# Exchanging two ScalarE instructions in the first chunk: square root of tile 2 ahead of tile 1's second-half evacuation

## The chip, the cores and the metric

The kernel runs on one core of one Trainium2 chip. The metric is the device time of one execution in microseconds (us). The six executions of the kernel before that the result is measured against lie between 180.17 and 180.61 us, within 0.24% of one another. The effect studied here is about that size (0.34%), so the experiments were timed in five rounds against the kernel before on the same chip, and the trace was read as well as the clock. The granted clock is the share of full speed that the profile records for TensorE; its mean is listed with every execution.

Engines: TensorE (PE in the profile; PEld is its weight load), VectorE (DVE), ScalarE (ACT), GpSimd (POOL), SyncE (SP).

## The reference

```
xn  = layernorm(x)                                    # x: 1 x 2048 x 512, bf16
A   = S5 state-space layer on xn (complex scan over 2048 steps)
B   = (silu(xn @ w_gate) * (xn @ w_up)) @ w_down      # hidden width 1376
out = x + A(xn) + B(xn)
```

The kernel takes the 2048 rows in four chunks of 512. Only the start of the first chunk matters here. Its four tiles of 128 rows (tile 0 to tile 3) are normalised and transposed, and TensorE multiplies each with the gate weights as soon as it is ready.

## The kernel before

The program records tasks in a graph, and a static list scheduler orders the tasks of ScalarE, VectorE and GpSimd from estimates of their durations. TensorE and SyncE keep the order in which they were recorded. Each engine is then given its list in that order. An `order` (`od`) entry constrains the scheduler only. It adds no semaphore, since it joins tasks of one engine.

For each tile, VectorE computes the statistics, ScalarE takes the square root of the variance, and VectorE takes the reciprocal and normalises in two halves of 256 columns:

```python
def ln_stat0(a, order):
    t = g.add("dve", lambda e: e.bn_aggr(out=mv[:, a, :], ...))
    hold["sd%d" % a] = g.add("act", lambda e: e.activation(out=sd0[:, a:a + 1], in_=mv[:, a, 1:2], func=AF.Sqrt, bias=epst[:, 0:1]), ...)
...
# VectorE's order in chunk 0: r reciprocal, n normalise half h, b statistics of half h, s aggregate (and ScalarE's square root)
for op, a, h in (("r", 0, 0), ("n", 0, 0), ("b", 1, 0), ("b", 1, 1), ("s", 1, 0), ("n", 0, 1), ("b", 2, 0),
                 ("r", 1, 0), ("n", 1, 0), ("n", 1, 1), ("b", 2, 1), ("s", 2, 0), ("b", 3, 0),
                 ("r", 2, 0), ("n", 2, 0), ("n", 2, 1), ("b", 3, 1), ("s", 3, 0), ...
```

Each half tile is transposed by TensorE into PSUM (line 569 of the program) and brought back to SBUF by ScalarE (line 581), or by VectorE for tile 3. The gate matmuls (line 785) read it there. The transposes are interleaved with the matmuls of the previous half:

```python
for q in range(4):                                   # q: tile
    for k0, k1 in ...((0, 2), (2, 4)):               # half of the contraction
        for n, (i, bk) in enumerate(tiles):          # seven gate tiles
            if k0 == 0 and n == (2 if q == 0 else 1):
                xt_tile_fine(q, 1)                   # two transposes, then evacuation ev<q>1
            if k0 == 2 and n == 1 and q < 3:
                xt_tile_fine(q + 1, 0)               # two transposes, then evacuation ev<q+1>0
            ...                                      # two matmuls of 128 columns
```

ScalarE's own order in this stretch is written out. `sd` is a square root and `ev` an evacuation, with tile and half:

```python
seq = ["sd0", "ev00", "sd1", "ev01", "ev10", "ev11", "sd2", "ev20", "sd3", "ev21"]
for a_, b_ in zip(seq, seq[1:]):
    hold[b_].od.add(hold[a_])
```

## Time and profile before

| | before |
|---|---|
| median of 3 runs | 180.33 us (180.17 to 180.47) |
| span in the profile | 178.5 us |
| TensorE, VectorE, ScalarE busy | 98%, 91%, 49% |
| TensorE's share of the chain that ended last | 97% |

The first two lines are from the profile's page: busy time by engine, and the shares of the chain that ended last, by engine.

```profile
PE 174.5 (98%) x936; PEld 83.8 (47%) x936; DVE 163.1 (91%) x285; ACT 87.5 (49%) x110; POOL 11.3 (6%) x21
...
PE 97%; ACT 1%; DVE 0%; issue 0%
```

So in this kernel a microsecond saved on VectorE or ScalarE should be worth nothing unless TensorE waits for it. TensorE's waits fit in three lines. One of them belongs here (engine, line, releaser: total us, times, longest):

```profile
PE pb L569 <- DVE xn_sb L514: 0.5, 1, 0.5
```

The chain of waits of the kernel before, around that place (start, duration, what):

```profile
8.10 0.13 PE pb L569 x2
...
8.24 0.38 ACT xnT L581
8.63 0.19 ACT sd L521
...
8.84 0.18 DVE rstd L529
...
9.04 0.36 DVE xn_sb L514
...
9.45 0.28 PE pb L569 x2
9.73 0.78 PE pb L785 x14
```

The chain leaves TensorE at 8.24, passes through ScalarE twice and VectorE twice, and comes back at 9.45. After that it stays on TensorE until the last output addition at 176.19. The same stretch in the timeline, and its last output addition (start, duration, engine, line, operation; in brackets the engine's idle time just before and its releaser):

```profile
7.50 0.21 DVE L519 BATCH_NORM_AGGREGATE mv<-st 128x2 f32<-128x12 f32 x1
...
7.93 0.28 PE L569 MATMUL pb<-ident,xn_sb 128*128 128x128 bf16 x2
...
8.24 0.38 ACT L581 ACTIVATE xnT<-pb 128x256 bf16<-128x256 bf16 x1 [0.57 <-PE pb L569]
8.52 0.29 ACT L521 ACTIVATE sd<-mv,epst 128x1 f32<-128x1 f32 x1
8.84 0.17 DVE L529 RECIPROCAL rstd<-sd 128x1 f32<-128x1 f32 x1 [0.84 <-ACT sd L521]
9.04 0.60 DVE L514 TENSOR_SCALAR xn_sb<-x_sb,mv,rstd 128x256 bf16<-128x256 bf16 x2
...
9.45 0.28 PE L569 MATMUL pb<-ident,xn_sb 128*128 128x128 bf16 x2 [0.46 <-DVE xn_sb L514]
...
10.35 0.28 PE L569 MATMUL pb<-ident,xn_sb 128*128 128x128 bf16 x2
...
176.19 0.29 DVE L958 TENSOR_TENSOR x_sb<-pb,x_sb 128x128 bf16<-128x128 f32 x1 [0.15 <-PE pb L953]
```

Tile 2's variance is complete at 7.50 + 0.21 = 7.71 us, but its square root (line 521) starts only at 8.52. Nothing in its own data holds it there. It stands in ScalarE's list behind the evacuation (the copy from PSUM to SBUF) at 8.24, which must wait for transposes that TensorE started at 7.93.

The cost is read from the starts of the transposes. From 9.45 to 10.35 TensorE needed 0.90 us for two transposes and 14 matmuls. From 7.93 to 9.45 it needed 1.52 us for the same work. The stall is therefore 0.62 us, although the list of waits counts 0.5: it counts from the modelled end of the matmul before, and in the records matmuls overlap (those of line 785 last 0.22 us each, but the 16 of a step start 0.90 / 16 = 0.056 us apart).

### The profile page before, as it was taken

To read this page: it belongs to the slowest core of one execution; us is meant where nothing else is said; L and a number is where in the kernel's file an instruction comes from. 1 tells how busy PE (TensorE), PEld (TensorE's weight loads), DVE (VectorE), ACT (ScalarE), POOL (GpSimd) and SP (SyncE) were. 2 spreads that over 40 slices of the span, in tenths; PEclk is the share of its full clock that TensorE was granted. 3 is DMA by queue.
4 is the path that set the end of the run, shared out by engine and by line. 5 is a ranking of instruction groups with operands and counts; after the bars stand their busy time and mean duration, and the time that the engine had idled before them with its cause. 6 is when DMAs were issued, how large, how long until landed. Compare 5 with 4: busy or idle time off the path is not lost.

```text
span 178.5 us, 2422 instructions
## 1 busy us (share of the span) xinstructions
PE 174.5 (98%) x936; PEld 83.8 (47%) x936; DVE 163.1 (91%) x285; ACT 87.5 (49%) x110; POOL 11.3 (6%) x21
## 2 busy tenths in 40 slices
PE   8989999999999999999999999999999999999994
PEld 2785444444444444444444444444444444444743
DVE  2768988997999999999999999999899999999933
ACT  4459999799999765024565651000965620000000
POOL 3014200130000000260000000000000000000000
PEclk9999999999999999999999999999999999999999
DMA  5995563569450000001510000001000000001022
GB/s 169 376 326 118 119 121 119 128 133 333 131 94 0 0 0 0 0 29 62 123 26 0 0 0 4 0 29 59 29 0 4 0 0 0 0 0 49 14 88 88
DMA packets 22978, 12.37 MB, mean 69 GB/s; under 512 B 15192, under 2 KB 22968, under 8 KB 22968
## 3 DMA queue, kind: packets, MB, share of 16 engines
q1 hardware_dynamic: 22472, 11.54, 23.6%
q10 hardware_dynamic: 496, 0.69, 1.1%
q8 instruction: 7, 0.11, 0.3%
q14 instruction: 3, 0.02, 0.0%
HBM read 6.46 MB, written 2.10 MB: 48 GB/s over the span
## 4 chain that ended last, share of the span: by engine, by line
PE 97%; ACT 1%; DVE 0%; issue 0%
PE pb L743 35%; PE pb L940 21%; PE pb L953 16%; PE pb L857 15%; PE pb L785 3%; PE pb L474 2%; PE pb L820 2%; PE pb L830 1%; PE pb L569 1%; ACT xnT L581 0%; DVE xn_sb L514 0%; DVE x_sb L958 0%; ACT sd L521 0%; DVE rstd L529 0%; PE pb L566 0%
## 5 line engine op out<-in xcount | busy, mean ns | idle before, releaser
L897 DVE TENSOR_TENSOR_SCAN rot<-sm,car,rot 128x512 bf16<-128x512 f32 x32 | 39.0, 1267 | 0.1
L940 PE MATMUL pb<-wd,hT 128*128 128x512 bf16 (+3 forms) x198 | 38.8, 356 | 0.0
L743 PE MATMUL pb<-xnT,wu 128*128 128x512 bf16 x160 | 37.3, 379 | 0.0
L743 PE MATMUL pb<-xnT,wg 128*128 128x512 bf16 x132 | 31.3, 380 | 0.0
L953 PE MATMUL pb<-W,hss 128*128 128x512 bf16 (+2 forms) x144 | 28.3, 356 | 0.0
L857 PE MATMUL pb<-xnT,BT 128*128 128x512 bf16 x128 | 28.1, 379 | 0.0
L940 PEld LDWEIGHTS pb<-wd,hT 128*128 128x128 bf16 (+1 forms) x198 | 18.5, 97 | 19.9
L755 ACT ACTIVATE sg<-pb 128x1024 bf16<-128x1024 f32 x20 | 20.1, 1024 | 9.2 <-PE pb L743 8.1
L743 PEld LDWEIGHTS pb<-xnT,wu 128*128 128x128 bf16 x160 | 15.6, 98 | 18.9 <-issue 0.2
L810 ACT ACTIVATE uf<-pb 128x1024 bf16<-128x1024 f32 x20 | 20.5, 1027 | 7.2 <-PE pb L743 6.1
L953 PEld LDWEIGHTS pb<-W,hss 128*128 128x128 bf16 x144 | 13.4, 98 | 14.3
L743 PEld LDWEIGHTS pb<-xnT,wg 128*128 128x128 bf16 x132 | 12.7, 98 | 15.7 <-issue 0.4
L857 PEld LDWEIGHTS pb<-xnT,BT 128*128 128x128 bf16 x128 | 12.5, 98 | 15.1
L864 ACT ACTIVATE u_sb<-pb 128x1024 bf16<-128x1024 f32 x16 | 16.2, 1021 | 5.9 <-PE pb L857 5.5
L958 DVE TENSOR_TENSOR x_sb<-pb,x_sb 128x512 bf16<-128x512 f32 (+2 forms) x18 | 11.1, 623 | 3.5 <-PE pb L953 3.5
L812 DVE TENSOR_TENSOR hT<-sg,uf 128x1024 bf16<-128x1024 bf16 x20 | 13.5, 684 | 0.6 <-ACT uf L810 0.5
L503 ACT ACTIVATE xn_sb<-x_sb,nmr,rstd 128x512 bf16<-128x512 bf16 x8 | 6.0, 803 | 9.7 <-DVE nmr L500 9.7
L839 ACT ACTIVATE sg<-pb 96x1024 bf16<-96x1024 f32 x2 | 2.0, 1020 | 17.1 <-PE pb L820 17.1
L888 DVE TENSOR_TENSOR rot<-u_sb,cosT 128x2048 bf16<-128x2048 bf16 x8 | 9.8, 1221 | 0.4 <-ACT u_sb L864 0.4
L888 DVE TENSOR_TENSOR rot<-rot,cosT 128x2048 bf16<-128x2048 bf16 x8 | 9.7, 1217 | 0.1
L888 DVE TENSOR_TENSOR rot<-u_sb,sin 128x2048 bf16<-128x2048 bf16 x8 | 9.8, 1220 | 0.0
L888 DVE TENSOR_TENSOR rot<-rot,sin 128x2048 bf16<-128x2048 bf16 x8 | 9.7, 1217 | 0.0
(78 smaller groups left out, 143.1 us busy)
## 6 DMA issues: line engine op xcount, KB each, us to landing
out_dram<-x_sb SPq DMA_DIRECT2D x15, 128.0 KB, 1.7
x_sb<-in_A_x_dram SPq DMA_DIRECT2D x3, 512.0 KB, 7.3
wd<-in_B_w_down_dram SPq DMA_DIRECT2D x1, 1280.0 KB, 6.8
wu<-in_B_w_up_dram SPq DMA_DIRECT2D x1, 768.0 KB, 5.0
wu<-in_B_w_up_dram SPq DMA_DIRECT2D x1, 608.0 KB, 7.2
x_sb<-in_A_x_dram SPq DMA_DIRECT2D x4, 128.0 KB, 3.4
wg<-in_B_w_gate_dram SPq DMA_DIRECT2D x1, 480.0 KB, 6.0
wg<-in_B_w_gate_dram ACTq DMA_DIRECT2D x1, 448.0 KB, 3.7
```

The source lines that it names most:

```text
L503: g.add("act", lambda e, a=a: e.activation(out=xn_sb[:, a % NXN, :], in_=x_sb[:, a, :], func=AF.Identity, scale=rstd[:, a:a + 1], bias=nmr ...
L743: inst = e.matmul(pbank[0:fs, bk, :].rearrange("p (j t) -> p j t", j=4), lhsT=w[:, kt, i * 128:i * 128 + fs], rhs=xnT[:, c % 2, :, kt, :], ...
L755: g.add("act", lambda e: e.activation(out=sg[rows, sl, 0:n, :].rearrange("p a t -> p (a t)"), in_=pair_f32(rows, bk, 512 * n), func=AF.Sil ...
L810: g.add("act", lambda e: e.activation(out=uf[rows, ul, 0:n, :].rearrange("p a t -> p (a t)"), in_=pair_f32(rows, bk, 512 * n), func=AF.Ide ...
L812: g.add("dve", lambda e: e.tensor_tensor(out=hT[rows, hb, i0:i0 + n, :], in0=sg[rows, sl, 0:n, :], in1=uf[rows, ul, 0:n, :], op=ALU.mult), ...
L857: inst = e.matmul(pbank[:, bk, :].rearrange("p (j t) -> p j t", j=4), lhsT=BT[:, ri, kt, pt * 128:(pt + 1) * 128], rhs=xnT[:, c % 2, :, kt ...
L864: g.add("act", lambda e: e.activation(out=u_sb[:, us].rearrange("p r t -> p (r t)"), in_=pair_f32(slice(0, 128), b0), func=AF.Identity), r ...
L888: tt = lambda out, a, b, op, r, w, nm: g.add("dve", lambda e: e.tensor_tensor(out=out, in0=a, in1=b, op=op), reads=r, writes=w, name="%s_% ...
L897: g.add("dve", lambda e, A0=A0, A1=A1, k=k, ri=ri, pt=pt: e.tensor_tensor_scan(out=A1[:, k, ri, :], data0=rr[:, pt:pt + 1].to_broadcast([1 ...
L940: inst = e.matmul(pbank[:, bk, 0:nc_], lhsT=hT[0:fs, hb, i, lt * 128:(lt + 1) * 128], rhs=wd[0:fs, i, c0:c0 + nc_], start=(i == 0), stop=F ...
L953: inst = e.matmul(pbank[:, bk, 0:nc_], lhsT=hss[:, hb, pt, ri, lt * 128:(lt + 1) * 128], rhs=W12[:, ri, pt, c0:c0 + nc_], start=False, sto ...
L958: g.add("dve", lambda e, bk=bk, a=a, c0=c0, nc_=nc_: e.tensor_tensor(out=x_sb[:, a, c0:c0 + nc_], in0=pbank[:, bk, 0:nc_], in1=x_sb[:, a, ...
```

## The change

The intent is to let ScalarE do first what can start first, namely the square root of tile 2 in the gap before the evacuation.

```diff
-            seq = ["sd0", "ev00", "sd1", "ev01", "ev10", "ev11", "sd2", "ev20", "sd3", "ev21"]
+            seq = ["sd0", "ev00", "sd1", "ev01", "ev10", "sd2", "ev11", "ev20", "sd3", "ev21"]
```

The scheduler sees other estimated times because of it and also moves some small work between 13 and 33 us. On VectorE three small operations and a piece of table arithmetic move; on ScalarE a sine table goes ahead of a Silu, and tiny sine evaluations change places. TensorE, GpSimd and SyncE keep their order. The diff of the source doesn't show these moves; they come from comparing the scheduled instruction lists.

## The prediction

> **What bounds the kernel now.** TensorE. The page gives it 174.5 of 178.5 us busy (98%), and the chain of waits that ended last is 97% TensorE, unbroken from 9.45 us to 176.17 us. VectorE is 91% busy, ScalarE 49%. The granted clock is 1.00 in every stretch. Its last detour is the one that the change touches: evacuation of tile 1's second half (ScalarE, 8.24), square root of tile 2 (8.52), reciprocal (VectorE, 8.84), normalisation of tile 2's first half (9.04), its transposes on TensorE (9.45).
>
> **The stall, from the timeline.** Transposes start at 6.98, 7.93, 9.45, 10.35, 11.24 us. A half-step without waiting (two transposes, 14 matmuls of 128 columns) therefore takes 0.89 to 0.90 us, 56 ns a matmul[...]. The step 7.93 to 9.45 took 1.52 us: 1.52 - 0.90 = 0.62 us of stall. (The list of waits counts 0.46 us, from the modelled end of the last matmul.)
>
> **What the change does.** No work is removed or added; two ScalarE instructions swap. Tile 2's variance is ready at 7.71, ScalarE is idle from 7.67 to 8.24, and the square root stands behind an evacuation that needs transposes begun at 7.93. Steps measured for the other tiles: aggregate start to square root start 0.24, to reciprocal 0.32, to normalisation 0.20, to transposes 0.40. From the aggregate at 7.50:
> - square root 7.74 (before 8.52), done by about 8.03 and so before the evacuation's 8.24, which is not delayed (0.29 us long in the trace);
> - reciprocal 8.06, normalisation 8.26, transposes possible from 8.66. TensorE reaches them at 7.93 + 0.90 = 8.83, so the stall vanishes entirely.
>
> Next link, tile 3: statistics 8.78, aggregate 9.24, square root 9.48 (behind an evacuation at 9.14), normalisation 10.00, transposes possible 10.40; TensorE arrives at 10.62. No new stall.
>
> **Does it survive?** From 9.45 on TensorE waits for nothing, so the 0.62 us should carry to the end unless something with less slack is fixed in time. Chunk 1's input landing (13.77) is fixed, and VectorE's statistics and the DMA transposes queue behind it. But TensorE needs the second weight transpose (landed about 22.1) only at 25.14; the last scaled weights (70.7) at 75.5; the last chunk's states (166.3) at 169.0. All slacks exceed 0.62 us. The static scheduler also reorders small work between 13 and 33 us (a few small VectorE products earlier, one table step ahead of chunk 1's normalisation, one sine table ahead of a Silu); I expect no effect on time, since chunk 1's DMA transpose stays bound by its queue at 22.2 us.
>
> **Prediction.** 180.33 - 0.62 = 179.7 us; 8 in 10: 179.45 to 180.05. Faster by over 2%: 0.01; within 2%: 0.985; slower: 0.005.
>
> **What would show it.** Square root of tile 2 near 7.74; transposes near 8.83 with no TensorE wait for the normalised tile; the later transposes spaced 0.90; feed-forward matmuls starting near 13.3 instead of 13.92; first Silu near 12.9; chunk 1's statistics still near 13.77; span near 177.9.
>
> **What would make it wrong.** Tile 3's chain arriving after 10.62, giving part back (its estimated margin is 0.22 us); the evacuation delayed by the square root; the reordered sine or table step delaying a Silu or a PSUM release and stalling TensorE between 14 and 30 us; DMA arrivals that TensorE now meets 0.62 us too early.

The 0.89 to 0.90 us of a half-step are read from the trace. The queue that holds chunk 1's DMA transpose to 22.2 us is in the trace: SyncE issued DMA transposes at 13.98, 18.11 and 22.23 us, and before the second and the third it waited 2.1 and 2.0 us for the landing of the one before.

## The result

| | before | after |
|---|---|---|
| median of 6 runs | 180.30 us (180.17 to 180.61) | 179.64 us (179.53 to 180.06) |
| ratio | | 0.9966 (95%: 0.9952 to 0.9981) |
| span in the profile | 178.5 us | 177.8 us |
| tile 2's first transposes after tile 1's last | 1.52 us | 0.89 us |
| first 512-column matmul starts | 13.92 us | 13.20 us |

A ratio is the mean time of one kernel's runs over that of the other's of the same rounds, so it is not quite the ratio of the medians quoted. The difference is clear of noise, and inside the 2%.

The page of the kernel after, the same two lines:

```profile
PE 173.5 (98%) x928; PEld 83.8 (47%) x936; DVE 163.1 (92%) x285; ACT 87.5 (49%) x110; POOL 9.2 (5%) x21
...
PE 95%; DMA 1%; DVE 1%; issue 0%; ACT 0%
```

The smaller TensorE share of the chain is no new wait. In this execution the eleven matmuls of a constant that TensorE runs first (line 474) ran shorter (3.78 instead of 4.21 us), so the chain begins at the first input's DMA and not with them. TensorE also shows 928 matmul records instead of 936, with 936 weight loads in both; eight are missing from the trace.

The timeline of the kernel after, for the lines shown of before:

```profile
7.42 0.21 DVE L519 BATCH_NORM_AGGREGATE mv<-st 128x2 f32<-128x12 f32 x1
...
7.67 0.29 ACT L521 ACTIVATE sd<-mv,epst 128x1 f32<-128x1 f32 x1
...
7.85 0.28 PE L569 MATMUL pb<-ident,xn_sb 128*128 128x128 bf16 x2
...
7.99 0.16 DVE L529 RECIPROCAL rstd<-sd 128x1 f32<-128x1 f32 x1
8.16 0.38 ACT L581 ACTIVATE xnT<-pb 128x256 bf16<-128x256 bf16 x1 [0.20 <-PE pb L569]
8.19 0.60 DVE L514 TENSOR_SCALAR xn_sb<-x_sb,mv,rstd 128x256 bf16<-128x256 bf16 x2
...
8.74 0.28 PE L569 MATMUL pb<-ident,xn_sb 128*128 128x128 bf16 x2
...
9.63 0.28 PE L569 MATMUL pb<-ident,xn_sb 128*128 128x128 bf16 x2
...
175.48 0.29 DVE L958 TENSOR_TENSOR x_sb<-pb,x_sb 128x128 bf16<-128x128 f32 x1 [0.15 <-PE pb L953]
```

The whole execution starts 0.08 us earlier (7.85 for 7.93), because the first input landed earlier (the first statistics start at 3.08 and not at 3.17). With that taken off, the square root moved from 8.52 to 7.75. The evacuation that it overtook runs from 8.16, which is 8.24 on the old scale: not delayed at all. The transposes of tile 2 follow those of tile 1 by 8.74 - 7.85 = 0.89 us, and the next two by 0.89 again. The chain of waits no longer leaves TensorE here:

```profile
8.01 0.11 PE pb L569 x2
8.12 0.78 PE pb L785 x14
8.90 0.11 PE pb L569 x2
9.02 0.78 PE pb L785 x14
```

The list of TensorE's waits still has a line of the same name:

```profile
PE pb L569 <- DVE xn_sb L514: 0.3, 1, 0.3
```

It is another instance. The timeline shows that this is tile 0's, at the start, where the shorter run of those first matmuls exposed a wait that was there before:

```profile
4.96 0.28 PE L569 MATMUL pb<-ident,xn_sb 128*128 128x128 bf16 x2 [0.35 <-DVE xn_sb L514]
```

A group in a list of waits is a line of the program, not one place in time.

### The profile page after: what moved, and what is told of

It reads as the page before. It is cut to its first block, busy times and chain, and to the rows that moved or that the text cites. A ratio compares the mean times of both kernels' runs of the same rounds, so it can differ in the third digit from the quotient of the medians.

```text
span 177.8 us, 2415 instructions
## 1 busy us (share of the span) xinstructions
PE 173.5 (98%) x928; PEld 83.8 (47%) x936; DVE 163.1 (92%) x285; ACT 87.5 (49%) x110; POOL 9.2 (5%) x21
## 4 chain that ended last, share of the span: by engine, by line
PE 95%; DMA 1%; DVE 1%; issue 0%; ACT 0%
PE pb L743 36%; PE pb L940 21%; PE pb L857 16%; PE pb L953 15%; PE pb L785 4%; PE pb L820 2%; DMA x_sb<-in_A_x_dram 1%; PE pb L830 1%; PE pb L569 1%; DVE st L527 0%; ACT xnT L581 0%; DVE xn_sb L514 0%; ACT sd L521 0%; DVE x_sb L958 0%; DVE mv L519 0%
## 5 line engine op out<-in xcount | busy, mean ns | idle before, releaser
L940 PE MATMUL pb<-wd,hT 128*128 128x512 bf16 (+3 forms) x194 | 38.1, 355 | 0.2
L743 PEld LDWEIGHTS pb<-xnT,wg 128*128 128x128 bf16 x132 | 12.7, 98 | 15.7 <-issue 0.8
```

The source lines that it names most:

```text
L743: inst = e.matmul(pbank[0:fs, bk, :].rearrange("p (j t) -> p j t", j=4), lhsT=w[:, kt, i * 128:i * 128 + fs], rhs=xnT[:, c % 2, :, kt, :], ...
L940: inst = e.matmul(pbank[:, bk, 0:nc_], lhsT=hT[0:fs, hb, i, lt * 128:(lt + 1) * 128], rhs=wd[0:fs, i, c0:c0 + nc_], start=(i == 0), stop=F ...
```

## The experiments

Theory: before the change TensorE stalled 0.62 us at tile 2, because the square root stood behind a later-ready evacuation. The exchange removes exactly that stall, and since TensorE bounds the rest, all of it reaches the end.

Rival 1: the gain comes from the work that the scheduler moved at 13 to 33 us. Rival 2: a delay at 8 us is partly absorbed by later slack, and the agreement of 0.62 us is an accident.

Experiments 1 to 4 ran on one chip in the same rounds, 5 to 8 on one, and 9 to 11 on one. All results were correct.

### 1. The exchange alone

```diff
+ # the kernel before, after scheduling:
+ act = streams["act"]
+ i, j = act.index(hold["ev11"]), act.index(hold["sd2"])
+ assert abs(i - j) == 1
+ act[i], act[j] = act[j], act[i]
```

> The kernel before with the square root of tile 2 and the evacuation of tile 1's second half exchanged after scheduling, so that nothing else moves on any engine. Theory (the 0.62 us stall of TensorE is removed and the gain carries): 0.62 us less than before, ratio 0.9966, transposes of tile 2 at about 0.90 us after those of tile 1's second half instead of 1.52. Rival (the gain comes from the small work that the scheduler moved between 13 and 33 us): ratio 1.000.

Measured: 179.61 us median against 180.35, ratio 0.9968 (0.9952 to 0.9985). Five runs lie between 179.55 and 179.77, and one is at 180.67. The timeline of this run (square root, then the two transposes in question):

```profile
7.67 0.29 ACT L521 ACTIVATE sd<-mv,epst 128x1 f32<-128x1 f32 x1
...
7.86 0.27 PE L569 MATMUL pb<-ident,xn_sb 128*128 128x128 bf16 x2
...
8.76 0.28 PE L569 MATMUL pb<-ident,xn_sb 128*128 128x128 bf16 x2
```

The step is 0.90 us. The exchange without any of the scheduler's moves gives the whole gain.

### 2. The scheduler's moves alone

```diff
+ # the same four lines, in the kernel after: the two instructions exchanged back
```

> The kernel after with those two ScalarE instructions exchanged back after scheduling, so that only the scheduler's later moves remain. Theory: the time of before, ratio 1.000 within 0.0010, stall of 0.62 us back. Rival (the later moves give the gain): ratio 0.9966.

Measured: 180.41 us against 180.35, ratio 1.0009 (0.9993 to 1.0025). The timeline:

```profile
8.08 0.28 PE L569 MATMUL pb<-ident,xn_sb 128*128 128x128 bf16 x2
...
9.59 0.28 PE L569 MATMUL pb<-ident,xn_sb 128*128 128x128 bf16 x2 [0.46 <-DVE xn_sb L514]
```

The stall is back (1.51 us, with its 0.46 us wait), and so is the time. Rival 1 falls.

### 3. The square root one place earlier still

```diff
- ScalarE: ... ev10, sd2, ev11 ...        (kernel after)
+ ScalarE: ... sd2, ev10, ev11 ...
```

> The kernel after with the square root one place earlier still, ahead of the evacuation of tile 1's first half. Theory (what counts is the order in which ScalarE's inputs become ready): the square root can't start before about 7.7 us, so the evacuation behind it starts about 0.7 us late, near 8.0 us, and TensorE stalls about 0.7 us there; the gain is lost, 180.3 to 180.5 us, ratio 1.000 to 1.001. Rival (the earlier the square root is issued the better): no loss, ratio 0.9966.

Measured: 180.20 us against 180.35, ratio 0.9992 (0.998 to 1.0004); most of the gain is gone. The timeline:

```profile
7.00 0.28 PE L569 MATMUL pb<-ident,xn_sb 128*128 128x128 bf16 x2
...
7.76 0.29 ACT L521 ACTIVATE sd<-mv,epst 128x1 f32<-128x1 f32 x1 [0.88 <-DVE mv L519]
7.96 0.36 ACT L581 ACTIVATE xnT<-pb 128x256 bf16<-128x256 bf16 x1
...
8.38 0.29 PE L785 MATMUL pb<-xnT,wg 128*128 128x128 bf16 x2 [0.38 <-ACT xnT L581]
...
8.51 0.28 PE L569 MATMUL pb<-ident,xn_sb 128*128 128x128 bf16 x2
```

The square root can't start before its variance is there (7.76), so the evacuation of tile 1's first half, which had been ready much earlier, starts at 7.96 behind it. TensorE waits for it, and the step from tile 1's first to its second transposes is 1.51 us instead of the 0.95 us that it took in before and after. That is a stall of 0.56 us. The expected 0.7 us of stall was somewhat too much: the evacuation started 0.96 us after its transposes instead of 0.31 (7.29 - 6.98 before), so it was 0.65 us late, of which 0.56 us reached TensorE. So "earlier" isn't the rule. The list has to follow the order in which inputs become ready.

### 4. Before, with a delay ahead of the square root

```diff
  ScalarE: ... ev11,
+          activation(Identity) of 512 columns into a scratch buffer,
           sd2 ...
```

> The kernel before with one useless ScalarE instruction of 512 columns between the evacuation and the square root of tile 2, which occupies ScalarE for about 0.52 us. Theory (in before every delay of this square root reaches the end of the kernel one for one): 0.52 us more, ratio 1.0029. Rival (part of a delay at 8 us is absorbed in later slack): less than half of that, ratio under 1.0015.

Measured: 180.72 us against 180.35, ratio 1.0019 (1.0006 to 1.0032). The medians are 0.37 us apart where 0.52 was expected. In the trace the added instruction held ScalarE for 0.52 us (8.56 to 9.08), the square root moved from 8.52 to 9.08, and the step between the transposes grew from 1.52 to 2.03 us, so the delay was there in full. In this kernel the scheduler had also moved an index computation on GpSimd, so it wasn't quite a single change. The interval allows both readings. It is taken up again in 9 and settled from the traces after 11.

### 5. The kernel after again

No edit; it is there to be compared with 6, 7 and 8 in the same rounds.

> The changed kernel itself, on the same chip and in the same rounds as the three runs beside it. Theory: ratio 0.9966 again, about 0.6 us less than before.

Measured: 179.54 us (179.49 to 179.64) against 180.33, ratio 0.9957 (0.9945 to 0.9969). This is a little more than expected: 0.79 us between medians on this chip.

### 6. After, with a short delay on VectorE

```diff
+ # after scheduling, ahead of tile 2's reciprocal; reads tile 2's square root
+ e.tensor_scalar(out=dlyb[:, 0:64], in0=iot[:, 0:64], scalar1=sd0[:, 2:3], scalar2=None, op0=ALU.add)
```

> The kernel after with one useless VectorE instruction of 64 columns between the square root and the reciprocal of tile 2 (about 0.1 to 0.15 us, an estimate from the small VectorE operations in the trace). Theory (tile 2's chain now has about 0.15 us of slack before TensorE comes for it: 8.59 against 8.74 us in the trace of after): no loss beyond 0.05 us against after, ratio 0.9966 to 0.9969 against before. Rival (tile 2's chain still bounds the kernel after the change): the whole delay shows, ratio about 0.9973.

Measured: 179.65 us median against 179.54 for the kernel after. Four runs are at 179.60 to 179.66, the others at 180.05 and 180.70. Those two pull the ratio to 0.9975 (0.9957 to 0.9992), so here it can't tell the readings apart. The profiled execution is the one at 180.05 (its timeline; line numbers are one higher from here on):

```profile
6.41 0.43 DVE L510 BATCH_NORM_STATS2 st<-x_sb 128x6 f32<-128x256 bf16 x1 [0.32 <-DMA x_sb<-in_A_x_dram]
...
8.15 0.29 ACT L522 ACTIVATE sd<-mv,epst 128x1 f32<-128x1 f32 x1
...
8.30 0.28 PE L570 MATMUL pb<-ident,xn_sb 128*128 128x128 bf16 x2
...
8.64 0.16 DVE L530 RECIPROCAL rstd<-sd 128x1 f32<-128x1 f32 x1
...
9.24 0.29 PE L570 MATMUL pb<-ident,xn_sb 128*128 128x128 bf16 x2
```

From square root to reciprocal is 0.49 us, against 0.32 in the kernel after, so the delay was 0.17 us. The step between the transposes is 0.94 us instead of 0.89, so 0.05 us shows. The square root was also 0.03 us later against tile 1's transposes than in the kernel after, and 0.17 + 0.03 less the expected slack of 0.15 gives just that. Tile 2 has slack now, but little. (The four undisturbed runs lie about 0.1 us above 179.54, between the two expectations.) The first line explains why this execution was late: VectorE waited 0.32 us for the DMA of tile 2's input, ahead of tile 1's reciprocal in its list, and everything shifted. That wait (6.41) lies before the instruction that was added (8.47). Whether the other late executions (180.67 in 1, 181.32 in 2, 180.70 here) had the same cause is open, as they left no trace.

### 7. After, with a long delay on VectorE

```diff
+ # the same with two operations of 512 columns, the second waiting for the first
```

> The same with two useless VectorE instructions of 512 columns, which wait for one another: about 0.8 us. Theory: the delay less the slack of 0.15 us, so 0.65 us more than after, all of the gain gone, ratio 1.000 against before within 0.001, and transposes of tile 2 about 1.55 us after those of tile 1's second half. Rival (no sensitivity, the gain came from elsewhere): ratio 0.9966.

Measured: 180.28 us (180.26 to 180.41) against 179.54 for after and 180.33 for before; ratio to before 0.9999 (0.9987 to 1.0011). The timeline:

```profile
7.99 0.28 PE L570 MATMUL pb<-ident,xn_sb 128*128 128x128 bf16 x2
...
8.06 1.01 DVE L1020 TENSOR_SCALAR dlyb<-iot,sd 128x512 f32<-128x512 f32 x2
...
9.58 0.29 PE L570 MATMUL pb<-ident,xn_sb 128*128 128x128 bf16 x2 [0.53 <-DVE xn_sb L515]
```

In the same trace the square root starts at 7.73 and the reciprocal at 8.98, 1.25 us apart against 0.32 in the kernel after, so the delay was 0.93 us; the 0.8 expected was an estimate. The stall is back by another road (1.59 - 0.89 = 0.70 us; the other 0.23 is the slack of 0.15 and the 0.08 us by which the square root came earlier against tile 1's transposes than in the kernel after), and the time rises by 0.74 us. The exchange is undone in its effect without touching ScalarE's order. So the stall of TensorE counts, and not the order as such.

### 8. Before, with a long delay on ScalarE

```diff
  ScalarE: ... ev11,
+          four activations(Identity) of 512 columns, each waiting for the last,
           sd2 ...
```

> The kernel before with four useless ScalarE instructions of 512 columns ahead of the square root of tile 2, each waiting for the last: about 2.45 us (3 times 0.65 and 0.52). Nothing else moves on any engine. Theory (one for one): 2.45 us more, ratio 1.0136. Rival (part of a delay at 8 us is absorbed later, as the 0.37 us measured for 0.52 us may suggest): 70% of it, 1.7 us, ratio 1.0095.

Measured: 184.45 us against 180.33, ratio 1.023 (1.0217 to 1.0243): 4.12 us and not 2.45. Neither expectation holds. The delay itself was near the expected: the four instructions held ScalarE from 8.54 to the square root at 11.05, 2.51 us. The longest wait of TensorE in this kernel, and TensorE in stretches of its own trace (stretch: length, busy time and matmuls, granted clock, DMA share, GB/s):

```profile
PE pb L570 <- DVE xn_sb L515: 3.0, 1, 3.0
```

```profile
8.90:11.90 3.00, 0.11 (x2) 1.00 1.09 359
11.90:12.40 0.50, 0.43 (x7) 0.88 1.12 356
...
12.70:15.40 2.70, 2.70 (x28) 0.50 0.10 30
...
15.50:15.70 0.20, 0.20 (x5) 0.52 0.83 197
15.70:20.00 4.30, 4.30 (x51) 1.00 0.58 129
```

In this trace TensorE stood idle for 3.0 us, up to 11.97, and soon after it had resumed its granted clock fell to 0.50 and stayed there for about 3.4 us. (The first stretch of mixed clock, mean 0.88 over 0.5 us, puts the fall at about 12.3; the stretch from 15.50 to 15.70, mean 0.52, puts the recovery just before 15.7.) Within it two transposes and 14 matmuls took 15.11 - 13.40 = 1.71 us, against 0.90 in the kernel before. Working at a clock of 0.50 for 3.4 us loses some 1.7 us, and 2.45 + 1.7 = 4.15 us, which is close to the 4.12 us measured. (The 1.7 is an estimate from those two figures; the trace gives 1.63, as shown after 11.) All five runs had the lower mean clock (0.990 or 0.991), and the other four left no trace. Why the clock fell, and why it came back when it did, isn't shown; 9 to 11 only try shorter delays.

### 9. One delay, with all other lists fixed

```diff
  ScalarE: ... ev11,
+          one activation(Identity) of 512 columns (inserted after scheduling, so nothing else moves),
           sd2 ...
```

> The kernel before with one useless ScalarE instruction (0.52 us) ahead of the square root of tile 2, this time with the other engines' streams exactly as before. Theory (one for one): 0.52 us more, ratio 1.0029. Rival (the earlier 0.37 us was real absorption): 0.37 us or less, ratio 1.0021 or less.

Measured: 180.85 us (180.80 to 181.09) against 180.30. The medians are 0.55 us apart, where 0.52 was expected. In these rounds one of eleven runs of the kernel before took 182.63 us with a mean clock of 0.991. It widens the interval of the ratio (1.0016, 0.9976 to 1.0057) beyond use, so 9, 10 and 11 are read from medians and single runs.

### 10. Two delays

```diff
+ # as in 9, with two
```

> Two such instructions, 1.17 us. Theory (one for one while the granted clock stays at 1.00): 1.17 us more, ratio 1.0065, TensorE idle about 1.6 us before tile 2's transposes. Rival (absorption at 70%): 0.82 us, ratio 1.0045.

Measured: 181.76 us (181.44 to 182.03) against 180.30; medians 1.46 us apart, lowest runs 181.44 - 180.22 = 1.22 us apart. Expected was 1.17. The clock was 1.00 in all five runs. The ratio, 1.0062 (1.0021 to 1.0104), carries the outlier of before. More than the delay was lost here, not less. In the profiled execution, the fastest of the five, the step grew from 1.52 to 2.69 us, which is the expected 1.17. The spread of these runs is wider than usual, and what made the other four longer stays open, as they left no trace.

### 11. Three delays

```diff
+ # as in 9, with three
```

> Three such instructions, 1.82 us, TensorE idle about 2.3 us. Four cost 4.1 us where 2.45 us was expected, because the granted clock fell to 0.50 for some 3.3 us after an idle time of 2.96 us. Theory: either the clock stays at 1.00 and it costs 1.82 us (ratio 1.0101), or it falls in some or all executions and those cost about 1.6 us more (ratio 1.019). Rival (the excess of four has nothing to do with the clock and grows evenly with the delay): about 3.0 us, ratio 1.0166, with the clock at 1.00.

Measured: two kinds of run. Two at 182.22 and 182.37 us had a mean clock of 1.00. Four at 183.51 to 183.79 us had 0.990 or 0.991. The ratio over both kinds is 1.0153. The first kind is 1.9 to 2.1 us above before's median for a delay of 1.82 us; the second is about 1.3 us above the first. In the profiled execution (182.37 us, clock 1.00) TensorE waited 2.3 us (the first two added instructions start 0.65 us apart, at 8.82 and 9.47) and the step grew by 1.84 us, from 1.52 to 3.36; the rest is a late start, as shown below.

Together, by the length of TensorE's idle time in the one profiled execution of each (in 11, one that kept the clock): at 1.6 us the mean clock was 1.00 in all five runs, at 2.3 us it was 0.990 or 0.991 in four of six, at 3.0 us in all five. In the runs whose mean clock was 0.999 or 1.00, delays of 0.52, 1.17 and 1.82 us cost 0.55, 1.46 and about 2.0 us. The 0.37 us of experiment 4 was not repeated when only the delay was changed.

The traces decide it more sharply than these medians. From the start of tile 2's first transposes to the start of the last output addition it took 166.73 to 166.75 us in all twelve traced executions whose mean clock was 1.00 (0.999 in 7), that is before, after, 1 to 7 and 9 to 11: 176.19 - 9.45 and 175.48 - 8.74 are both 166.74, and so are 176.74 - 10.00 in experiment 4 and 177.36 - 10.62 in 10. Whatever happened to tile 2 before that point reached the end in full, so rival 2 (absorption) falls. In 8 it took 180.34 - 11.97 = 168.37 us: the stretch at a clock of 0.50 cost 1.63 us. With the growth of the step, 4.02 - 1.52 = 2.50 us, this makes 4.13 of the 4.12 us measured.

In the traced executions the scatter that is left lies before the change: tile 1's second transposes started anywhere from 7.85 to 8.30 us (3 left aside, where the edit itself delays them). In 6 the input of tile 2 was late. In 9 and 11 (8.27 and 8.23) TensorE's first four gate matmuls and the two transposes after them took 0.61 and 0.62 us (5.88 to 6.49 and 5.94 to 6.56), where the kernel before took 0.39 (5.89 to 6.28); why isn't shown, and the recorded clock of 1.00 doesn't show it. In 11 the late start of 0.30 us and the delay of 1.84 us account for all of the 2.1 us by which this execution is longer than the profiled one of before (182.37 - 180.24).

## Why the prediction was right

- **Size.** Predicted 180.33 - 0.62 = 179.7 us; measured 179.64. The ratio 0.9966 is 0.61 us. The exchange alone gave the same (1), and the later moves alone gave nothing (2).
- **Stall.** Predicted: it vanishes. The step went from 1.52 to 0.89 us, the time that the work itself needs.
- **Steps of tile 2.** Predicted square root 7.74, reciprocal 8.06, normalisation 8.26, transposes 8.83. Measured 7.67, 7.99, 8.19 and 8.74, each 0.07 to 0.09 us earlier, as was the execution as a whole. The intervals measured on other tiles could simply be carried over.
- **The overtaken evacuation is not delayed.** It started 0.31 us after the transposes it reads, as before (8.16 - 7.85, 8.24 - 7.93).
- **Tile 3's margin.** Predicted 0.22 us. In the kernel after, its normalisation starts at 9.93, so transposes are possible at 10.33 with the measured 0.40 us, and TensorE came at 10.53: 0.20 us.
- **Carrying to the end.** The first 512-column matmul came 0.72 us earlier and the last output addition 0.71 us earlier (175.48 for 176.19), of which 0.08 us is the earlier start, a matter of chance between two executions. Nothing was lost in between, as the slacks listed in the prediction had said. Chunk 1's statistics stayed where their DMA holds them (13.77 before, 13.82 after).
- **What the prediction didn't have.** It took a stall on TensorE to cost its own length. That holds for the 0.62 us here, but not in experiment 8, where the trace has 3.0 us of idle time and the time rose by 4.12 us for 2.50 us of longer step, nor in the four runs of 11 with a mean clock of 0.990 or 0.991, which took 3.2 to 3.5 us more than before's median for a delay of 1.82 us (the traced run of 11, with 2.3 us of idle time, kept 1.00). One run of the kernel before, without any added delay, took 182.63 us with a mean clock of 0.991. It left no trace, so its cause isn't shown.

In the trace of the kernel after, TensorE waits for no other engine after 5.81 us. Two waits before that, of 0.35 and 0.34 us, remain, and no run tried to shorten them.

## What to carry to other kernels

When an engine that takes its list in order serves two chains, as ScalarE did here (in experiment 3 the evacuation started at 7.96, behind the square root that waited until 7.76), list its instructions by the time at which their inputs are ready. One that is ready early and feeds a chain to the bottleneck engine loses by standing behind one that is ready late, and placing it too early only moved the stall to the other chain (0.56 us in experiment 3). Measure such a stall by the starts of equal pieces of work on the bottleneck engine, and expect its whole length back, but no more, if that engine never waits afterwards and its recorded clock stays the same (here 0.62 us of stall and 0.61 us of time, at a clock of 1.00). Look at what a scheduler moves besides, and test it separately, before it gets credit or blame.
